# Newton's S as 32 moving columns, B's forms from PSUM, and k's DMA transpose ahead of C's transpose

## The chip, the cores and the metric

The kernel runs on one core of a Trainium2 chip. The metric is device time in microseconds (us); every time is the median of several executions, with the lowest and highest where they matter. A program on one core has one span per execution. The profile is of one execution, and the span of an execution is about 2 us shorter than its time (269.7 and 271.84 in the profiled one of the kernel before).

Short names: PE is the matmul engine (TensorE), PEld its weight loads, DVE is VectorE, ACT is ScalarE, POOL is GpSimd, SP issues DMA.

## The reference

Eight batches of eight heads, 576 tokens, head size 64. Attention in Nystrom form with 32 landmarks, then a gated feed-forward stage:

```python
q_lm = q.reshape(B, H, m, S // m, D).mean(axis=3)        # m = 32 landmarks
k_lm = k.reshape(B, H, m, S // m, D).mean(axis=3)
A, Bm, C = sm(q, k_lm), sm(q_lm, k_lm), sm(q_lm, k)      # sm: scaled softmax
Z = Bm.transpose(0, 1, 3, 2) / (norm1(Bm) * norm_inf(Bm) + 1e-06)
for _ in range(6):
    Z = 2 * Z - Z @ Bm @ Z                               # Newton
x = A @ Z @ C @ v                                        # then heads side by side: 4608 x 512
out = (1 / (1 + exp(-(x @ w_gate))) * (x @ w_val)) @ w_out   # d_ff = 1536
```

## The kernel before

Attention's work of batch b+1 is woven into the feed-forward matmuls of batch b (tiles gp, vp, then op). Who decides the weave matters for all that follows: while the program is built, a small model of the engines' times (class Model in the kernel) says when each piece's data will be there, and a loop puts the next piece on the PE when the model says that it is due. On the chip the order is fixed; if the model was wrong, PE stands at the matmul that it put too early.

```python
def start(self, engine, outs, ins):
    return max([self.free[engine]] + [self.landed.get(_handle(x), 0.0) for x in ins]
               + [self.waits.get(_handle(x), 0.0) for x in outs])
...
# in weave(): the first stream whose data the model has ready now; else the one that is ready first
now = model.free["pe"] + SLACK
...
SLACK, LAG, FILL = 0.02, 20, 1.0
```

The model knows when an operand has landed, when its engine is free and when a bank's former user is done. It does not know that two engines may not use one PSUM bank at once.

In a late batch (2 to 7) B's softmax ran from exponentials in SBUF (E), was transposed on VectorE, and spread into block-diagonal form (bd, bdT), four heads of 32 in 128 columns:

```python
E = sb.tile([128, 2, m], FP32, name=f"E_{b}", tag="E")
act.activation(out=E, in_=bs, func=AF.Exp, scale=scale2)
... # rs = row sums of E, rr = 1 / rs
act.mul(out=Bc[:, g, :], in_=E[:, g, :], mul=rr[:, g:g + 1])
dve.transpose(out=Bt, in_=Bc)
... # spread(dst, src): dst[:, g] = blk * src[:, g], broadcast over the four heads
spread(bdT, Bt)
... # s0 = bdT' bdT per group g, 128 columns
spread(bd, Bc)
```

Newton moves the square S (128 columns, three quarters of them zeros) and y (64) together through PE, and one VectorE operation makes the next pair:

```python
for it in range(ITERS):
    lo = 0 if it < ITERS - 1 else 128
    yield need(sy, banks=1)
    pn = bank([128, 2, 128 + D - lo], FP32, f"pn_{b}_{it}")
    for g in range(2):
        mm(out=pn[:, g, :], lhsT=sy[:, g, 0:128], rhs=sy[:, g, lo:128 + D], ...)
    dve.scalar_tensor_tensor(out=nsy, in0=sy, scalar=2.0, in1=pn, op0=ALU.mult, op1=ALU.subtract)
```

From batch 3 on k and q are transposed by DMA, and so is C (tile ct, from cl). Before, k's transpose of the next batch was issued after C's transpose of this one.

The softmax here doesn't subtract the row's maximum and nothing guards it: scores larger than these inputs give would overflow.

## Time and profile before

| | before |
|---|---|
| time | 271.59 us, median of 3 (271.58 to 271.88) |
| span in the profile | 269.7 us |
| granted TensorE clock | 0.998 |
| PE, DVE, ACT busy | 96%, 72%, 59% |

The busy shares and the chain that ended last are shown in the prediction. In the chain the first column is the start in us and the second the length; in the groups the two numbers after the bar are busy us in all and mean ns of one, and the last is the idle time of that engine just before them.

### The profile page before, as it was taken

How to read it: one execution, taken by the hardware profiler on the slowest of the kernel's cores; microseconds unless marked ns; L12 is line 12 of the kernel's file. 1: busy time of each engine (PE TensorE's matmuls, PEld its weight loads, DVE VectorE, ACT ScalarE, POOL GpSimd, SP SyncE). 2: the span in 40 equal slices, each digit the busy share in tenths (PEclk: the TensorE clock that was granted, in tenths of full speed). 3: DMA queues.
4: the chain of work that ended last, by engine and by line, in shares of the span. 5: the costliest groups of instructions: out<-in, count | busy, mean ns of one | idle time of the engine just before them, and what ended most of it. 6: DMA issues, size and time to landing. Idle time of an engine off the chain costs nothing.

```text
span 269.7 us, 8019 instructions
## 1 busy us (share of the span) xinstructions
PE 260.1 (96%) x3089; PEld 167.0 (62%) x3123; DVE 193.3 (72%) x551; ACT 159.4 (59%) x413; POOL 96.2 (36%) x107
## 2 busy tenths in 40 slices
PE   8999999999999999999999999999999999999994
PEld 5877777757664666556646665556636664665443
DVE  4566888976899788948986778848968786963111
ACT  3663876866647754876477655875368643964001
POOL 8523231960874039511953078212922000000000
PEclk9999999999999999999999999999999999999999
DMA  6999999999795998889794989589530413101433
GB/s 94 193 206 205 205 206 206 205 203 172 141 194 115 204 170 121 181 135 199 141 221 72 182 157 203 129 139 199 124 90 12 97 41 80 41 0 41 117 103 92
DMA packets 62645, 38.00 MB, mean 141 GB/s; under 512 B 33552, under 2 KB 58128, under 8 KB 62608
## 3 DMA queue, kind: packets, MB, share of 16 engines
q0 software_dynamic: 23600, 18.88, 47.0%
q1 hardware_dynamic: 38896, 18.52, 31.4%
q8 instruction: 24, 0.39, 0.6%
q14 instruction: 13, 0.11, 0.1%
q10 hardware_dynamic: 112, 0.10, 0.1%
HBM read 37.75 MB, written 9.44 MB: 175 GB/s over the span
## 4 chain that ended last, share of the span: by engine, by line
PE 93%; ACT 2%; issue 2%; POOL 1%; DVE 0%; POOLq 0%; ACTq 0%
PE op L247 34%; PE gp L247 18%; PE vp L247 18%; PE idle_ps L247 3%; PE pn L247 2%; PE cv L247 2%; PE rb L247 2%; PE sc L247 1%; PE sa L247 1%; PE tp_q L252 1%; PE up_1g L247 1%; PE up_0g L247 1%; PE up_2g L247 1%; PE tp_k L252 1%; PE up_1v L247 1%
## 5 line engine op out<-in xcount | busy, mean ns | idle before, releaser
L247 PE MATMUL op<-wo_sb,ht 128*128 128x512 bf16 (+1 forms) x410 | 109.4, 373 | 2.1 <-issue 1.1
L153 ACT ACTIVATE th<-gp 128x288 bf16<-128x288 f32 x192 | 76.7, 415 | 48.4 <-PE gp L247 36.7
L153 DVE SCALAR_TENSOR_TENSOR ht<-th,vp 128x288 bf16<-128x288 bf16 x192 | 82.0, 448 | 21.9 <-ACT th L153 17.2
L247 PE MATMUL gp<-an,U 128*128 128x288 bf16 x384 | 78.5, 286 | 0.3
L247 PE MATMUL vp<-an,V 128*128 128x288 bf16 x384 | 78.4, 286 | 0.0
L247 PEld LDWEIGHTS <-ht 128*128 128x128 bf16 x444 | 39.9, 98 | 26.7 <-issue 5.8
L247 PEld LDWEIGHTS <-U 128*128 128x128 bf16 x384 | 35.9, 98 | 27.3 <-issue 2.5
L247 PEld LDWEIGHTS <-V 128*128 128x128 bf16 x384 | 37.5, 98 | 9.7 <-issue 0.2
L153 ACT ACTIVATE ob<-op 128x512 f32<-128x512 f32 (+1 forms) x31 | 18.2, 587 | 29.6 <-PE op L247 24.2
L153 DVE SCALAR_TENSOR_TENSOR sy<-sy,pn 128x384 bf16<-128x384 bf16 x35 | 19.2, 548 | 2.3 <-PE pn L247 1.9
L153 DVE TENSOR_SCALAR ob<-op 128x512 f32<-128x512 f32 (+2 forms) x7 | 4.2, 596 | 17.3 <-PE op L247 17.3
L247 PE MATMUL idle_ps<-idle_w 128*128 128x256 bf16 x86 | 14.8, 308 | 1.2 <-DVE idle_w L297 1.2
L247 PE MATMUL pn<-sy 128*128 128x192 bf16 (+1 forms) x84 | 13.1, 237 | 0.4 <-ACT kT L153 0.3
L153 DVE TENSOR_TENSOR an<-aexp,rb 128x384 bf16<-128x384 bf16 (+1 forms) x32 | 12.4, 446 | 0.3 <-PE rb L247 0.3
L247 PEld LDWEIGHTS <-sy 128*128 128x128 bf16 x88 | 8.1, 97 | 6.2 <-DVE sy L153 2.8
L153 ACT ACTIVATE aexp<-sa 128x288 bf16<-128x288 f32 x32 | 10.7, 418 | 1.5 <-PE sa L247 1.1
L247 PEld LDWEIGHTS <-idle_w 128*128 128x128 bf16 x86 | 8.5, 109 | 3.3 <-DVE idle_w L297 1.2
L247 PEld LDWEIGHTS <-WT 64*32 64x32 bf16 x384 | 3.8, 89 | 9.1 <-issue 6.6
L270 POOL DMA_DIRECT2D kn<-in_k_dram x9 | 7.0, 779 | 4.6 <-DMA wg_sb<-in_moe_w_gate_dram 2.1
L153 DVE CAST U<-up_0g 128x512 bf16<-128x512 f32 x8 | 5.5, 690 | 4.1 <-PE up_0g L247 4.1
L270 POOL DMA_DIRECT2D vn<-in_v_dram x8 | 6.3, 789 | 5.3 <-PE gp L247 4.5
L270 POOL DMA_DIRECT2D qn<-in_q_dram x9 | 6.8, 753 | 4.0 <-PE sm L247 2.2
(201 smaller groups left out, 349.7 us busy)
## 6 DMA issues: line engine op xcount, KB each, us to landing
vn<-in_v_dram POOLq DMA_DIRECT2D x8, 576.0 KB, 9.4
kn<-in_k_dram POOLq DMA_DIRECT2D x7, 576.0 KB, 8.1
qn<-in_q_dram POOLq DMA_DIRECT2D x7, 576.0 KB, 10.6
out_dram<-ob SPq DMA_DIRECT2D x53, 64.0 KB, 3.0
out_dram<-ob SPq DMA_DIRECT2D x17, 192.0 KB, 2.3
out_dram<-ob SPq DMA_DIRECT2D x18, 128.0 KB, 2.4
wg_sb<-in_moe_w_gate_dram POOLq DMA_DIRECT2D x3, 512.0 KB, 19.7
wv_sb<-in_moe_w_val_dram POOLq DMA_DIRECT2D x3, 512.0 KB, 21.0
```

What stands on the lines that cost most here:

```text
L153: f(**kw)
L247: nc.tensor.matmul(**kw)
L252: nc.tensor.transpose(**kw)
L270: nc.gpsimd.dma_start(out=t[:, hs], in_=src[b, hs].rearrange("h (p c) d -> p h (c d)", p=P6))
```

## The change

Three parts, all in the late batches (the third from batch 4 on). (1) Newton: only the 32 nonzero columns of S move, so a pair of pn matmuls has 96 columns each in place of 192; the price is that S must be spread again on VectorE after each step (sd), from a copy in PSUM (new). (2) B's forms: the exponentials stay in the PSUM tile bs, bd is made straight from them, and a matmul with a matrix of ones (four) replaces VectorE's transpose. (3) Queues: k's transpose by DMA and its sums on GpSimd come ahead of C's transpose of the batch before, and the loads move with them. A small piece more is in the edit: from batch 1 on the column maxima (cc) lie in the PSUM bank of n1. Every experiment that starts from the change keeps this piece and the constant four, so neither was tried alone.

```diff
+    COMPACT = 2
+    four = consts.tile([128, m], BF16, name="four")
...
-        for what in ("k", "q") if b >= TURN else ():
+        for what in ("k", "q") if TURN <= b <= SWAP else ():
+            yield from turned_by_dma(what)
         for what in ("k", "q"):
+            if b > SWAP:
+                if what == "q":
+                    yield made(turned_c, b - 1)
+                yield from turned_by_dma(what)
...
-        E = sb.tile([128, 2, m], FP32, name=f"E_{b}", tag="E")
+        late = b >= LATE
+        E = bs if late else sb.tile([128, 2, m], FP32, name=f"E_{b}", tag="E")
...
+        if late:
+            for g in range(2):
+                dve.scalar_tensor_tensor(
+                    out=bd[:, g], in0=E[:, g, None, :].to_broadcast([128, NP, m]),
+                    scalar=rr[:, g:g + 1], in1=blk, op0=ALU.mult, op1=ALU.mult)
+            yield need(bd, banks=1)
+            Bt = bank([128, 2, m], FP32, f"Bp_{b}")
+            for g in range(2):
+                mm(out=Bt[:, g], lhsT=bd[:, g], rhs=four, start=(g == 0), stop=(g == 1))
+        if b >= COMPACT:
+            Bs = sb.tile([128, 2, m], BF16, name=f"Bt_{b}", tag="Bt")
+            act.copy(out=Bs, in_=Bt)
...
-                    mm(out=pn[:, g, :], lhsT=sy[:, g, 0:128], rhs=sy[:, g, lo:128 + D],
+                    mm(out=pn[:, g, :], lhsT=sd[:, g], rhs=sy[:, g, lo:w + D],
...
+                        dve.scalar_tensor_tensor(
+                            out=new, in0=sy[:, :, 0:m], scalar=2.0, in1=pn[:, :, 0:m],
+                            op0=ALU.mult, op1=ALU.subtract)
...
+                        dve.tensor_mul(
+                            out=sd, in0=blk[:, None].to_broadcast([128, 2, NP, m]),
+                            in1=new[:, :, None, :].to_broadcast([128, 2, NP, m]))
...
-            if b > TURN:
+            if TURN < b <= SWAP:
                 yield made(turned_c, b - 1)
```

More of the change, by code (lines that the diff above doesn't have):

```diff
@@ L350 @@
     model.free["dve"], model.free["act"] = 5.4, 6.6
+    four = consts.tile([128, m], BF16, name="four")
+    nc.vector.tensor_reduce(
+        out=four, in_=ident.rearrange("p (i l) -> p l i", i=NP), axis=AX.X, op=ALU.max)
     front_of, sums_of, lm_of, value_of, mid_of, norm_of, an_of, uv_of, step_at = ({} for _ in range(9))
-    square_of, turned_c, q_of = {}, {}, {}
+    square_of, turned_c, q_of, sd_of = {}, {}, {}, {}
     def copy(out, in_):
@@ L410, in front, with turned_by_dma @@
         ends = {}
-        for what in ("k", "q") if b >= TURN else ():
+        def turned_by_dma(what):
             yield made(nat, (what, b))
@@ L419, in front @@
                 t, t.rearrange("p h (c x) -> p (h c) x", c=3), n, n.rearrange("p h d -> p (h d)"))
+        for what in ("k", "q") if TURN <= b <= SWAP else ():
+            yield from turned_by_dma(what)
         for what in ("k", "q"):
+            if b > SWAP:
+                if what == "q":
+                    yield made(turned_c, b - 1)
+                yield from turned_by_dma(what)
+                if what == "q" and b < B - 1:
+                    load(b + 1, "k")
             if b >= TURN:
@@ L454, in front @@
             pool.tensor_add(out=s2, in0=s1, in1=t[:, :, 2 * P6:3 * P6])
-            if b >= SWAP and what == "k" and b < B - 1:
+            if b == SWAP and what == "k":
                 load(b + 1, "k")
+                load(b + 1, "q")
+            elif b > SWAP and what == "q" and b < B - 1:
                 load(b + 1, "q")
@@ L610, in mid @@
                 act.mul(out=Bc[:, g, :], in_=E[:, g, :], mul=rr[:, g:g + 1])
-        Bt = sb.tile([128, 2, m], BF16, name=f"Bt_{b}", tag="Bt")
-        dve.transpose(out=Bt.rearrange("p g l -> p (g l)"), in_=Bc.rearrange("p g l -> p (g l)"))
         bdT = sb.tile([128, 2, NP, m], BF16, name=f"bdT_{b}", tag="bdT")
         bd = sb.tile([128, 2, NP, m], BF16, name=f"bd_{b}", tag="bd", bufs=3)
+        if late:
[7 more added lines that the diff above has]
+                mm(out=Bt[:, g], lhsT=bd[:, g], rhs=four, start=(g == 0), stop=(g == 1))
+        else:
+            Bt = sb.tile([128, 2, m], BF16, name=f"Bt_{b}", tag="Bt")
+            dve.transpose(out=Bt.rearrange("p g l -> p (g l)"), in_=Bc.rearrange("p g l -> p (g l)"))
+        if b >= COMPACT:
+            Bs = sb.tile([128, 2, m], BF16, name=f"Bt_{b}", tag="Bt")
+            act.copy(out=Bs, in_=Bt)
         def spread(dst, src):
+            if late:
+                return dve.tensor_mul(
+                    out=dst, in0=blk[:, None].to_broadcast([128, 2, NP, m]),
+                    in1=src[:, :, None, :].to_broadcast([128, 2, NP, m]))
             for g in range(2):
@@ L627, in mid @@
         yield need(model.landed[Bc.name] + (0.25 if b else 0.0), banks=1)
-        n1 = bank([128, 2, m], FP32, f"n1_{b}")
+        n1_cc = bank([128, 2 * m + 2], FP32, f"n1_{b}")
+        n1 = n1_cc[:, 0:2 * m].rearrange("p (g l) -> p g l", g=2)
         mm(out=n1, lhsT=blk, rhs=Bc, start=True, stop=(b > 0))
@@ L631, in mid @@
             mm(out=n1, lhsT=eps, rhs=idle_w[:, 0:2 * m], start=False, stop=True)
-        ce = sb.tile([128, 2], FP32, name=f"cc_{b}", tag="cc")
+        ce = n1_cc[:, 2 * m:] if b > 0 else sb.tile([128, 2], FP32, name=f"cc_{b}", tag="cc")
         dve.tensor_reduce(out=ce, in_=n1, axis=AX.X, op=ALU.max)
@@ L638, in mid @@
         dve.reciprocal(out=rc, in_=ce)
-        apart = 2 if b == 0 else 1
+        apart, w = 2 if b == 0 else 1, m if b >= COMPACT else 128
         yield need(bdT, banks=apart)
-        s0 = [bank([128, 2 // apart, 128], FP32, f"s0_{b}{x}") for x in range(apart)]
+        s0 = [bank([128, 2 // apart, w], FP32, f"s0_{b}{x}") for x in range(apart)]
         s0 = [s0[g % apart][:, g // apart] for g in range(2)]
         for g in range(2):
-            mm(out=s0[g], lhsT=bdT[:, g], rhs=bdT[:, g], start=(g == 0 or b == 0), stop=(g == 1 or b == 0))
-        sy = sb.tile([128, 2, 128 + D], BF16, name=f"sy_{b}_0", tag="sy0", bufs=2)
+            mm(out=s0[g], lhsT=bdT[:, g], rhs=Bs[:, g] if b >= COMPACT else bdT[:, g],
+               start=(g == 0 or b == 0), stop=(g == 1 or b == 0))
+        sy = sb.tile([128, 2, w + D], BF16, name=f"sy_{b}_0", tag="sy0", bufs=2)
         if b == 0:
             model.by_part.add(sy.name)
-        s_at = [each(b, g).mul(sy[:, g, 0:128], s0[g], rc[:, g:g + 1]) for g in range(2)]
+        s_at = [each(b, g).mul(sy[:, g, 0:w], s0[g], rc[:, g:g + 1]) for g in range(2)]
         if b == 0:
             square_of[b] = [(sy, s_at)]
-        spread(bd, Bc)
+        elif b >= COMPACT:
+            sd_of[b] = sb.tile([128, 2, NP, m], BF16, name=f"sd_{b}_0", tag="sd", bufs=2)
+            for g in range(2):
+                dve.scalar_tensor_tensor(
+                    out=sd_of[b][:, g], in0=s0[g][:, None, :].to_broadcast([128, NP, m]),
+                    scalar=rc[:, g:g + 1], in1=blk, op0=ALU.mult, op1=ALU.mult)
+        if not late:
+            spread(bd, Bc)
         aexp = sb.tile([128, 2, S], BF16, name=f"aexp_{b}", tag="aexp", bufs=2)
@@ L667, in scale_y @@
                 dve.tensor_mul(out=ysc, in0=rcs, in1=rc)
-                y_at = [each(b, g).mul(sy[:, g, 128:128 + D], cv[g], ysc[:, g:g + 1])
+                y_at = [each(b, g).mul(sy[:, g, w:w + D], cv[g], ysc[:, g:g + 1])
                         for g in range(2)]
@@ L671, in scale_y @@
                 y_at = [dve.tensor_scalar(
-                    out=sy[:, g, 128:128 + D], in0=cv[g], scalar1=rcs[:, g:g + 1],
+                    out=sy[:, g, w:w + D], in0=cv[g], scalar1=rcs[:, g:g + 1],
                     scalar2=rc[:, g:g + 1], op0=ALU.mult, op1=ALU.mult) for g in range(2)]
@@ L802, in newton @@
             sy, bd, _ = mid_of[b]
+            compact = b >= COMPACT
+            w = m if compact else 128
+            sd = sd_of.pop(b) if compact else sy[:, :, 0:128]
             y6 = sb.tile([128, 2, 2, D], BF16, name=f"y6_{b}", tag="y6")
             for it in range(ITERS):
-                lo = 0 if it < ITERS - 1 else 128
-                yield need(sy, banks=1)
-                pn = bank([128, 2, 128 + D - lo], FP32, f"pn_{b}_{it}")
+                last = it == ITERS - 1
+                lo = w if last else 0
+                yield need(sy, *((sd,) if compact else ()), banks=1)
+                p = bank([128, 2 * (w + D - lo) + 2 * m * (compact and not last)], FP32, f"pn_{b}_{it}")
+                pn = p[:, 0:2 * (w + D - lo)].rearrange("p (g x) -> p g x", g=2)
                 for g in range(2):
-                    mm(out=pn[:, g, :], lhsT=sy[:, g, 0:128], rhs=sy[:, g, lo:128 + D],
+                    mm(out=pn[:, g, :], lhsT=sd[:, g], rhs=sy[:, g, lo:w + D],
                        start=(g == 0), stop=(g == 1))
-                if lo == 0:
-                    nsy = sb.tile([128, 2, 128 + D], BF16, name=f"sy_{b}_{it + 1}", tag="sy", bufs=3)
+                if not last:
+                    if compact:
+                        new = p[:, 2 * (w + D):].rearrange("p (g x) -> p g x", g=2)
+                        dve.scalar_tensor_tensor(
+                            out=new, in0=sy[:, :, 0:m], scalar=2.0, in1=pn[:, :, 0:m],
+                            op0=ALU.mult, op1=ALU.subtract)
+                    nsy = sb.tile([128, 2, w + D], BF16, name=f"sy_{b}_{it + 1}", tag="sy", bufs=3)
                     dve.scalar_tensor_tensor(
                         out=nsy, in0=sy, scalar=2.0, in1=pn, op0=ALU.mult, op1=ALU.subtract)
+                    if compact:
+                        sd = sb.tile([128, 2, NP, m], BF16, name=f"sd_{b}_{it + 1}", tag="sd", bufs=2)
+                        dve.tensor_mul(
+                            out=sd, in0=blk[:, None].to_broadcast([128, 2, NP, m]),
+                            in1=new[:, :, None, :].to_broadcast([128, 2, NP, m]))
+                    else:
+                        sd = nsy[:, :, 0:128]
                     sy = nsy
@@ L820, in newton @@
                             out=y6[:, g],
-                            in0=sy[:, g, None, 128:128 + D].to_broadcast([128, 2, D]), scalar=2.0,
+                            in0=sy[:, g, None, w:w + D].to_broadcast([128, 2, D]), scalar=2.0,
                             in1=pn[:, g, None, :].to_broadcast([128, 2, D]),
```

## The prediction

> **What bounds the kernel now.** I read the page first, for the busy shares and the chain that ended last; then the sums by 10 us windows; then the chain piece by piece in one steady stretch; then TensorE's and VectorE's groups kept apart by shape; last the list of waits.
>
> ```profile
> span 269.7 us, 8019 instructions
> PE 260.1 (96%) x3089; PEld 167.0 (62%) x3123; DVE 193.3 (72%) x551; ACT 159.4 (59%) x413; POOL 96.2 (36%) x107
> PE 93%; ACT 2%; issue 2%; POOL 1%; DVE 0%; POOLq 0%; ACTq 0%
> ```
>
> The reader sees a TensorE kernel: PE is busy 96% and carries 93% of the chain. The other 7% lies nearly all before 50 us, where the first batch is being loaded and warming matmuls (idle_ps, 86 of them) fill the gaps. After that PE has no holes, as the chain shows around the sixth of eight batches:
>
> ```profile
> 131.07 0.43 PE op L247 x2
> 131.51 0.19 PE pn L247 x2
> 133.60 0.17 PE pn L247 x2
> 134.69 0.06 PE pn L247 x2
> 135.66 0.11 PE wtp L247 x2
> 136.70 0.34 PE up_0g L247 x8
> 137.04 0.22 PE up_0v L247 x8
> 138.78 0.97 PE op L247 x4
> 140.90 0.43 PE op L247 x2
> ```
>
> (These are picked lines of one stretch.) A pair of 512-column matmuls takes 0.43 us, a pair of 192 columns 0.17, of 128 columns 0.11, of 64 columns 0.06: PE runs at its streaming rate, about 0.42 ns a column, and the price of a matmul is its moving columns. The one other cost is a change between whole-array matmuls and those in 32-column tiles: the first group of eight after a change takes 0.34 us where the next takes 0.22, and four op take 0.97 after a change back where two pairs need 0.86. So each edge costs 0.11 to 0.12 us.
>
> Does PE wait for anybody in the loop that the change rewrites (Newton, tiles pn and sy)?
>
> ```profile
> PEld L247 <- DVE sy L153: 3.1, 12, 0.4
> DVE sy L153 <- PE pn L247: 1.9, 6, 0.7
> L247 PE MATMUL pn<-sy 128*128 128x192 bf16 x70 | 11.5, 246 | 0.4 <-ACT kT L153 0.3
> ```
>
> The weight loads wait 3.1 us in all, but the matmuls behind them see 0.4 us of idle: other work of the feed-forward stage lies between two Newton steps and hides the VectorE round trip. VectorE's groups that I use for sizes:
>
> ```profile
> L153 DVE SCALAR_TENSOR_TENSOR sy<-sy,pn 128x384 bf16<-128x384 bf16 x35 | 19.2, 548 | 2.3 <-PE pn L247 1.9
> L153 DVE TENSOR_TENSOR an<-aexp,rb 128x192 bf16<-128x192 bf16 x16 | 5.5, 346 | 0.0
> L153 DVE SCALAR_TENSOR_TENSOR y<-sy,pn 128x128 bf16<-128x128 bf16 x14 | 3.4, 283 | 0.9 <-PE pn L247 0.7
> L153 DVE STREAM_TRANSPOSE Bt<-Bc 128x64 bf16<-128x64 bf16 x8 | 2.0, 246 | 4.4 <-ACT Bc L153 4.3
> L153 DVE TENSOR_SCALAR sy<-s,rc 128x128 bf16<-128x128 f32 x15 | 4.6, 345 | 0.6
> ```
>
> **What the Trainium skill says.** "VectorE: DVE Perf Modes", section "Why PSUM operands drop a tier": a PSUM operand in fp32 leaves a two-tensor operation at one element a cycle. The trace agrees: 384, 192 and 128 elements in 548, 346 and 283 ns are close to 148 ns plus n/0.96. So I take 215 ns for 64 elements and 415 for 256. "TensorE: Matmul & The Clock Gate", section "Back-to-back issue gap", puts a floor of about 60 cycles (25 ns) under a matmul of up to 64 columns; the trace agrees (the 96 x 32 sums lm_0k and the 64-column pn both follow each other by about 28 ns), so a matmul of 32 columns is no cheaper than one of 64. "TensorEngine Tiling (Array Packing)", section "Key Properties", says that a change of tiling mode drains TensorE; the trace shows it as the 0.11 us edge above.
>
> **The change part by part.** On the PE, in columns.
> Newton: six batches (2 to 7) times five steps times two matmuls go from 192 to 96 columns. A pair cost 0.17 us and should cost 0.085: 30 pairs times 0.085 = 2.5 us saved. The sixth step stays at 64 columns.
> The starting square s0: six pairs of 128 columns (0.11) become pairs of 32 at the floor (0.06): 0.3 saved.
> B's transpose: six pairs with the new matrix of ones ("four"), 32 columns, at the floor: 6 x 0.06 = 0.35 added.
> Edges: I counted them in the order of the built programs, taking whole array, 64-row tiles and 96-row tiles as three modes: 94 before, 103 after (in the late batches C's scores now come with B's ahead of the up-projection, and the A scores and C's value product are no longer neighbours). 9 x 0.11 = 1.0 us added.
> Warming matmuls stay 86, and the order of batches 0 and 1 stays; the one extra reduction in the setup (about 0.25 us of VectorE) lies beside ScalarE's 1.16 us copy of sel, which the chain runs through. I count nothing for it.
> Sum on the path: -2.5 - 0.3 + 0.35 + 1.0 = -1.45 us.
>
> On VectorE, which is beside the path. A Newton step was one operation of 384 elements (548 ns, the next starting some 0.47 us after it). It becomes three: 64 elements into PSUM (215), which the next must wait for, then 192 (348) and 256 (415); with the overlap of the last two that is 0.85 us. 0.38 more, times 30 = 11.4 us. For B and s0 per batch: the transpose goes (-0.25), the two spreads become one of the same size, bd's two become slower ones from PSUM with a scalar (+0.2), s0's two get shorter (-0.2) and two new ones of 128 elements appear (+0.6): about 0.4, times 6 = 2.3. VectorE goes from 193 to about 207 us, 77% of the span. ScalarE takes six small copies, 1.4 us in all. None of this is on the path as long as PE has other work between two Newton steps.
>
> The moves on the queues (k's transpose and its GpSimd sums ahead of C's transpose, k's load behind q's transpose) make landmarks ready earlier. PE waits for none of that now, so the move by itself earns nothing; it lets the order put a batch's attention work every 26 us of PE work, where it was 29.5.
>
> **Rivals.**
> VectorE becomes the bound. For: per batch it had about 22 us of work in 29.5, and gets about 24 in 26, and during Newton it is nearly full already. Against: counted in the built order for batch 4, PE has 9.8 us of work between its first and last Newton pair (6.3 before), and VectorE about 10.2 (7.0 before): the ratio is better than before, where PE hardly waited. If it fails, each of six batches could stall PE by 0.5 to 1 us: 273 to 276.
> A transfer becomes the bound. For: the tighter period gives loads, transposes and the two half-swaps less time, and PE's order is fixed. Against: in batches 4 to 7 the queries' landmarks were ready about 2 us before the B scores that use them, and DMA is idle in much of the last third. One stall of 1 us in each late batch would give 273 or so.
> The round trip hides nothing and the PE saving is lost to the edges and small waits: 271 to 271.6, the same as before.
> A larger gain than the columns (below 268) would need waits that I cannot find after 50 us, or a shorter start; the start is not touched.
>
> **Range and chances.** 271.6 - 1.45 = 270.1; I add 0.3 for small waits at the longer Newton round trip: 270.4. The best case is about 269 (no edges felt, columns fully earned), a bad one 272.5, with one rival partly true. 8 in 10: 269.0 to 272.2. Faster by over 2% means below 266.2, which the columns cannot pay: 2%. Slower by over 2% means above 277, six stalls of a microsecond: 4%. The rest, 94%, is within 2%.
>
> **What would show it.** The pn pairs of late batches take 0.08 to 0.09 us in the chain, in place of 0.17; the busy time of pn falls by some 2 us or more; VectorE's busy time is near 207; the edges cost 0.11 each; the share of PE in the chain stays at 93%. I am wrong if PE shows idle before pn, bs or up in the late batches (VectorE or a transfer took over), if the new VectorE operation into PSUM takes much more than 0.22 us, or if the stretch before 50 us changes its length.

## The result, and the profile after

The changed kernel took 273.13 us (median of 4, 272.95 to 273.56), and the kernel before took 271.63 us (median of 4, 271.58 to 271.88) beside it. The ratio is 1.0056, with a 95% interval of 1.0038 to 1.0073: slower by half a per cent, within 2%, and above the predicted range. A ratio here is the mean time of one kernel's fast runs over that of the other's of the same rounds, so it is not quite the ratio of the medians.

First the head of the page of the changed kernel (span, busy time of the engines, shares of the chain by engine):

```profile
span 270.8 us, 8170 instructions
...
PE 263.0 (97%) x3135; PEld 164.3 (61%) x3135; DVE 201.4 (74%) x612; ACT 160.9 (59%) x419; POOL 96.2 (36%) x107
...
PE 89%; ACT 4%; DMA 3%; DVE 2%; issue 1%; POOL 1%; ACTq 0%; POOLq 0%
```

Two lines disagree at first sight: PE is busier, 97% against 96%, yet its share in the chain fell from 93% to 89%. The chain points the right way: between 50 us and the last gp it holds 11.3 us of ScalarE and VectorE, and none before. It is no measure of the loss, for PE worked through most of these 11.3 us; and its 3% of DMA is the first load of q, which took the place of other pieces before 10 us. The busy share misleads. A matmul's record lasts longer than its turn (rtp below has a record of 246 ns, and a matmul of its 128 columns follows the one before by 55 ns), so a wait of 0.2 us disappears under the tail of the matmul before it; besides, 34 of the 444 op matmuls had no record in the profile before and all have one here. The Trainium skill, "Perfetto Trace Analysis", section "Identifying the Most-Contended Engine", says that matmul busy share is no good measure of how close a kernel is to its limit; this pair of profiles agrees, since the share rises by a point while the kernel gets slower. So I compared the starts of the matmuls instead.

The groups of the changed kernel, kept apart by shape, show what the new pieces cost:

```profile
L153 DVE TENSOR_TENSOR sd<-blk,pn 128x256 bf16<-128x256 bf16 x30 | 12.4, 415 | 0.0
L153 DVE SCALAR_TENSOR_TENSOR sy<-sy,pn 128x192 bf16<-128x192 bf16 x30 | 10.6, 354 | 1.0
L153 DVE SCALAR_TENSOR_TENSOR pn<-sy,pn 128x64 f32<-128x64 bf16 x30 | 6.6, 222 | 0.1
L153 DVE SCALAR_TENSOR_TENSOR bd<-bs,rr,blk 128x128 bf16<-128x128 f32 x12 | 3.7, 346 | 3.6 <-ACT Bc L153 3.6
L249 PE MATMUL pn<-sy,sd 128*128 128x96 bf16 x60 | 7.5, 207 | 0.1
L254 PE MATMUL rtp<-ident,rhl 128*80 128x128 bf16 x8 | 2.0, 246 | 0.2
```

The first three rows are the new Newton step on VectorE, with close to the durations predicted (415, 348, 215 ns). The pn row has 7.5 us of busy time for 60 matmuls, where the wide one had 11.5 for 70 (ten of them, batch 1's, stay wide and take 1.7). The bd row is the surprise: VectorE stood 3.6 us in front of twelve operations, released by ScalarE's Bc, from which bd takes no data.

**Where the time went.** I took the start of every matmul from the two traces and put them against the order of the built program. Each matmul was given its columns at the streaming rate (2.38 columns a ns, at least 27 ns) and each change of tile mode 0.1 us; call the sum the work. What a stretch takes beyond its work is called lost. This is an estimate from the trace's own rates, the same for both kernels.

| us | before | after |
|---|---|---|
| PE work of the whole program | 251.4 | 249.9 |
| lost up to the end of batch 0's gp and vp | 10.05 | 10.06 |
| lost from there to the last gp of batch 7 | 4.10 | 6.79 |
| start of the last pair of gp | 245.31 | 246.50 |

The work fell by 1.5 us, as predicted. The loss in the start did not change. But 2.7 us more are lost in the steady part, and 2.7 - 1.5 = 1.2 is what the profiled run lost (1.19 at the last pair of gp, 1.1 in the span).

The largest single piece is at 65.9 us, in batch 2. The chain of the changed kernel there (start, length, what):

```profile
65.15 0.86 ACT cexp L153 x2
66.02 0.36 ACT Bc L153 x2
66.37 0.02 issue
66.40 0.04 DVE bd L153
66.43 0.23 issue
66.67 0.35 DVE bd L153
67.02 0.05 issue
67.07 0.19 PE Bp L249
```

and three lines of its timeline (what stands in brackets is the idle time of the engine before the line, and who ended it):

```profile
65.91 0.46 ACT L153 ACTIVATE Bc<-bs,rr 128x32 bf16<-128x32 f32 x2
...
66.40 0.61 DVE L153 SCALAR_TENSOR_TENSOR bd<-bs,rr,blk 128x128 bf16<-128x128 f32 x2 [0.88 <-ACT Bc L153]
...
66.81 0.45 PE L249 MATMUL Bp<-four,bd 128*128 128x32 bf16 x2 [0.50 <-DVE bd L153]
```

ScalarE has C's exponentials (cexp) to do first; its Bc comes after them. VectorE's bd reads the same PSUM tile bs, so the built program lets it wait for Bc, and PE's Bp waits for bd: 0.66 us at the first Bp by the starts and 0.23 at the second. The Trainium skill, "PSUM — Partial Sum Buffer", section "PSUM bank collisions raise a hardware error", says that the hardware doesn't arbitrate between two engines on one bank, reads included, and that they must be ordered by semaphores. The trace agrees in so far as the built program orders them: bd is released by ACT Bc six times (3.6 us in all), with no data between them. What happens without that order, no run here shows. The kernel's model does not know this, so it put Bp too early.

The other waits are small: 0.21 us at each of four row-sum transposes (rtp of batches 3 to 6), 0.19 before pn in two batches, 0.15 after n1 in two, 0.1 each in three other places. All that I can name add to 3.0 us after. Before they add to between 0.5 and 1.4, as some of its gaps may be missing records. The rest of the 6.8 and the 4.1 is spread too thin to name.

The chain at an rtp shows what these are made of:

```profile
97.49 1.01 ACT aexp L153 x3
98.50 0.31 ACT th L153
98.81 0.02 issue
98.83 0.04 DVE ht L153
98.87 0.34 issue
99.20 0.42 DVE sm L153
99.62 0.02 issue
99.65 0.21 DVE rhl L153
...
100.14 0.25 PE rtp L254
```

ScalarE does A's exponentials (aexp), then th; VectorE's next operation in line is ht, which needs th, and the row sums' reciprocal (sm) and rhl stand behind it. VectorE was idle for 1.27 us ahead of that ht:

```profile
98.83 0.46 DVE L153 SCALAR_TENSOR_TENSOR ht<-th,vp 128x288 bf16<-128x288 bf16 x1 [1.27 <-ACT th L153]
```

So VectorE is not full there: it stands in line for ScalarE. That points to the order; experiments have to show it.

### The profile page after: what moved, and what is told of

Same layout as the page of the kernel before. It is cut to its first block, busy times and chain, and to the rows that moved or that the text cites. A ratio compares the mean times of both kernels' runs of the same rounds, so it can differ in the third digit from the quotient of the medians.

```text
span 270.8 us, 8170 instructions
## 1 busy us (share of the span) xinstructions
PE 263.0 (97%) x3135; PEld 164.3 (61%) x3135; DVE 201.4 (74%) x612; ACT 160.9 (59%) x419; POOL 96.2 (36%) x107
## 4 chain that ended last, share of the span: by engine, by line
PE 89%; ACT 4%; DMA 3%; DVE 2%; issue 1%; POOL 1%; ACTq 0%; POOLq 0%
PE op L249 35%; PE gp L249 16%; PE vp L249 16%; DMA qn<-in_q_dram 3%; PE idle_ps L249 2%; ACT aexp L153 2%; PE pn L249 2%; PE rb L249 2%; PE sc L249 1%; PE tp_q L254 1%; PE sa L249 1%; PE up_0g L249 1%; PE up_2g L249 1%; PE up_1g L249 1%; PE cv L249 1%
## 5 line engine op out<-in xcount | busy, mean ns | idle before, releaser
L249 PE MATMUL op<-wo_sb,ht 128*128 128x512 bf16 (+1 forms) x444 | 112.7, 374 | 0.0
L153 DVE SCALAR_TENSOR_TENSOR ht<-th,vp 128x288 bf16<-128x288 bf16 x192 | 79.8, 449 | 19.1 <-ACT th L153 18.3
L249 PEld LDWEIGHTS <-ht 128*128 128x128 bf16 x444 | 39.9, 98 | 32.4 <-issue 7.1
L249 PEld LDWEIGHTS <-U 128*128 128x128 bf16 x384 | 35.0, 98 | 20.0 <-issue 0.8
L153 ACT ACTIVATE ob<-op 128x512 f32<-128x512 f32 (+1 forms) x29 | 17.1, 589 | 28.6 <-PE op L249 25.2
L153 DVE TENSOR_SCALAR ob<-op 128x512 f32<-128x512 f32 (+2 forms) x9 | 5.5, 616 | 19.8 <-PE op L249 19.8
L153 DVE SCALAR_TENSOR_TENSOR sy<-sy,pn 128x192 bf16<-128x192 bf16 (+1 forms) x35 | 13.3, 381 | 1.7 <-PE pn L249 0.7
L153 DVE TENSOR_TENSOR sd<-blk,pn 128x256 bf16<-128x256 bf16 x30 | 12.4, 415 | 0.0
L249 PEld LDWEIGHTS <-sd 128*128 128x128 bf16 x72 | 6.3, 98 | 7.9 <-DVE sd L153 2.4
L249 PE MATMUL pn<-sy,sd 128*128 128x96 bf16 (+1 forms) x72 | 8.9, 205 | 0.1
L153 ACT ACTIVATE cl<-sl 128x288 bf16<-128x288 f32 x20 | 7.9, 414 | 1.3 <-PE sl L249 1.1
```

The lines of the kernel that those rows point to most:

```text
L153: f(**kw)
L249: nc.tensor.matmul(**kw)
```

## The experiments

Three theories. The *order theory*: PE's order is fixed at build by the kernel's own model, the order before happened to fit the chip, and any part that moves the order loses time in small waits, whatever the part itself costs. The *VectorE theory* (the first rival of the prediction): the longer Newton step on VectorE makes PE wait, so kernels with VectorE's old load do not lose. The *transfer theory*: the moved transposes and loads come late. Under the last two the loss belongs to one part and goes with it. The expectations number them: theory 1 is the wait of bd for Bc on the shared PSUM tile, which the model doesn't know, 2 the VectorE theory, 3 the transfer theory, 4 the order theory.

Each edit is told against the changed kernel, save two against the kernel before. "Lost" is as defined above, from the profiled run, in the steady part (before 4.1, after 6.8); "work" is PE's. All runs gave correct results.

**One part left out.** Five rounds in one call; before 271.69 (271.46 to 272.86, 11 runs).

```diff
# e1_forms_as_before: B's forms as before
-        late = b >= LATE
+        late = False
-            Bs = sb.tile([128, 2, m], BF16, name=f"Bt_{b}", tag="Bt")
-            act.copy(out=Bs, in_=Bt)
+            Bs = Bt
# e2_wide_newton: Newton as before
-    COMPACT = 2
+    COMPACT = 99
# e3_queues_as_before: transposes and loads as before
-        for what in ("k", "q") if TURN <= b <= SWAP else ():
+        for what in ("k", "q") if TURN <= b else ():
-            if b > SWAP:
+            if False:
-            if TURN < b <= SWAP:
+            if TURN < b:
... # and both loads after k's sums
```

> B's forms as in the kernel before (exponentials in SBUF, VectorE's block transpose), narrow Newton and the new queue order kept. In the built order PE has 248.6 us of work by my count (249.9 in the change, 251.4 before) and 93 edges (103 in the change). Theory 1, VectorE's new block-diagonal B waits for ScalarE on a shared PSUM tile and PE's order does not know: the 0.9 us stall of batch 2 goes, with 1.3 us of work: about 270.9 us. Theory 2, VectorE is too full in the Newton stretch: only 0.4 us per batch leaves VectorE, the other stalls (about 1.9 us) stay, about 271.8 us.

> Newton's S with 128 columns and one VectorE operation a step as before; B's forms from PSUM and the new queue order kept. PE work by count 252.1 us (2.1 more than the change). Theory 1: batch 2's stall at B's transpose stays; about 275 us. Theory 2, VectorE too full: stalls of 2.3 us vanish with the 2 us per batch that leave VectorE: about 272.9 us, no slower than the change.

> Loads, transposes and their order as before; narrow Newton and B's forms from PSUM kept. PE work by count 249.0 us, 94 edges. Theory 1: batch 2's stall stays (its order is not touched by the queues), the small later ones too: 0.9 us less work, about 272.2 us. Theory 3, the tighter period that the queue order brings makes the later stalls: these (about 1.4 us) vanish too, about 270.8 us.

Measured: without the forms 272.05 us, ratio to before 1.0015 (0.9982 to 1.0048), lost 7.7; with wide Newton 276.34, ratio 1.0168 (1.0150 to 1.0187), lost 8.1; with the old queues 274.26, ratio 1.0096 (1.0073 to 1.0120), lost 9.4. Leaving out a part never brings the loss back to 4.1, and leaving out the narrow Newton or the queues makes the kernel slower than the whole change. The medians lie 0.25, 1.3 and 2.1 us above the highest time that any theory had expected for the three. Where the waits lie changes from kernel to kernel: without the forms 0.5 and 0.7 us stand ahead of B's and C's scores of batch 5 (bs and sl, behind a GpSimd operation, bq); with wide Newton 0.4 to 0.9 us stand at Bp in five batches (2 and 4 to 7) and 0.9 ahead of cv of batch 3. One wait does go with its part: the 0.9 us at Bp of batch 2 stand in the traces of all kernels with that batch's bd read from PSUM and the model not told (the change, e2, e3, e5), and in none of the others.

**The model told more.** In the same call, one kernel whose model is told of the shared tile and of a scalar column's cost. The instructions are the change's.

```diff
# e7_told
-            columns = sum(k in aps for k in ("scalar1", "scalar2", "mul"))
+            columns = sum(k in aps for k in ("scalar", "scalar1", "scalar2", "mul"))
+            model.waits[bd.name] = model.landed[Bc.name]
+                model.waits[bdT.name] = model.landed[Bs.name]
```

> The change with only its order of emission told the truth: the scheduler's model learns that VectorE's block-diagonal B starts after ScalarE's normalised B, that its spread starts after ScalarE's copy of the transpose, and that a scalar column costs 60 ns in the three-operand form. The instructions are the same, their order is not. PE work by count 248.9 us, 93 edges. Theory 1: the stalls at B's transpose vanish and about 1 us of work with them: about 271.0 us or a little less. Theory 2: VectorE's load is the same, stalls of about 2 us stay somewhere: 272.1 us or more.

Measured: 272.76 us, ratio 1.0044 (1.0015 to 1.0073), work 248.9, lost 8.6. Work fell by 1.0 because the new order has 93 mode changes in place of 103, but more is lost. The wait at Bp of batch 2 is gone, but others came (0.5 and 0.7 us between C's scores, for example). The model told three things does not give an order that fits better on the whole; telling it one of them is tried below.

**One part alone.** Four rounds; before 271.70 (271.28 to 275.87, 9 runs). The edits are pairs of those above: Newton alone is e1 and e3 together, the forms alone e2 and e3, the queues alone e1 and e2.

> Only the narrow Newton of the change; B's forms and the queues as before. PE work by count 249.1 us (2.3 less than before), VectorE 12 us more. Theory 2 (VectorE's load makes PE wait): about 2 us or more of waits, 271.3 us or more. Theory 4 (the order of before is finely fitted to the chip, and any change of the order brings waits of 2 to 5 us, whatever VectorE's load): the same here, 271.5 to 274; it is told apart by the next two, which have VectorE's load of before.

> Only B's forms from PSUM; Newton and queues as before. PE work by count 251.9 us (0.4 more), VectorE about 1 us more. Theory 1: the 0.9 us stall of batch 2 and smaller ones in later batches at B's transpose: about 273.2 us. Theory 2: no waits elsewhere. Theory 4: waits of 2 us or more, also at places without B's forms.

> Only the new order of loads and transposes; Newton and B's forms as before. PE work by count 251.2 us (0.2 less), VectorE's load as before. Theory 2: no new waits, 271.4 us. Theory 3 (the tighter period) and theory 4 (any new order): waits of 1 to 4 us, 272.5 us or more.

Measured: Newton alone 272.98 us, ratio 1.0042 (1.0021 to 1.0064), lost 7.6; the forms alone 275.30, ratio 1.0148 (1.0114 to 1.0181), lost 7.1; the queues alone 275.03, ratio 1.0127 (1.0092 to 1.0162), lost 8.5. Alone, the three cost 0.4, 1.5 and 1.3%, which is 3.2% in sum; together they cost 0.6%. They do not add, so most of the loss is not a fixed property of a part.

The queues alone lose time without VectorE's new work. The head of its page:

```profile
PE 263.3 (96%) x3123; PEld 168.5 (62%) x3123; DVE 193.1 (70%) x551; ACT 159.0 (58%) x414; POOL 96.0 (35%) x107
```

VectorE has exactly its old work (193 us, 551 instructions), and PE loses 4.4 us more than before. What it waits for most is a transfer. The view of the tile ct (C's transpose), first its own row, then what PE waited for ahead of cv, which reads it (us, times):

```profile
L389 SPq DMA_TRANSPOSE ct<-cl x5: 1428/1576/2242, 90.2 to 201.6; - x5
...
  DMA ct<-cl: 7.2, 4
```

and the same view of the changed kernel:

```profile
L389 SPq DMA_TRANSPOSE ct<-cl x5: 1466/1820/3136, 88.9 to 197.6; - x5
its engine sat idle before it (us, times) until:
  issue: 0.2, 1
```

(The 7.2 us are over weight loads and matmuls, so most of it is counted twice; by the starts, cv of batches 4 and 5 waits 1.45 and 2.18 us.) These two waits are 3.6 of the 4.4 us. From its issue to its landing the slowest ct takes 8.7 us here, 7.2 in the change and 5.1 before. That the moved queue is the reason is not shown: p1 below has the old queue, and a ct of 8.6 us. In the whole change PE does not wait at cv. So a late transfer is the loss of this kernel, and not that of the change.

**The wait of batch 2 taken away, same order.** If the shared PSUM tile makes bd wait, exponentials in SBUF free it. The order of instructions on all five engines is that of the change, so only the wait differs. One kernel does it in all late batches (in the call of "one part alone"), one in batch 2 only.

```diff
# e8_e_in_sbuf
-        E = bs if late else sb.tile([128, 2, m], FP32, name=f"E_{b}", tag="E")
+        E = sb.tile([128, 2, m], FP32, name=f"E_{b}", tag="E")
# g2_e_in_sbuf_batch_2
+        E = bs if late and b > 2 else sb.tile([128, 2, m], FP32, name=f"E_{b}", tag="E")
```

> The whole change, but with the exponentials of B in SBUF in place of PSUM, so that VectorE and ScalarE need not take turns on one PSUM tile. The order of the instructions stays the same on every engine, nothing else changes. Theory 1: VectorE no longer waits for ScalarE there and the 0.9 us at B's transpose in batch 2 shrinks to 0.3 or less: 0.6 to 0.9 us faster than the change, about 272.4 us. If the stall comes of ScalarE or VectorE being late anyway, no difference.

Measured: 274.07 us (273.07 to 276.51), ratio 1.0100 (1.0049 to 1.0151), lost 7.0. In batch 2 the wait is gone (lost from bs to the first pn 0.8 us in place of 1.5), but in batch 6 the same stretch loses 2.0 us in place of 0.7; a new wait of about 1 us stands at Bp there, which comes behind bd and a copy that stands in line after it. The timeline of this kernel shows why (VectorE and GpSimd):

```profile
169.87 1.64 POOL L153 TENSOR_TENSOR s_7k<-kT 128x768 f32<-128x768 bf16 x1 [2.65 <-DMA kT<-kn]
...
170.94 2.44 DVE L153 SCALAR_TENSOR_TENSOR bd<-E,rr,blk 128x128 bf16<-128x128 f32 x2
...
171.59 1.64 POOL L153 TENSOR_TENSOR s_7k<-s_7k,kT 128x768 f32<-128x768 f32 x1
```

and the second bd alone:

```profile
171.58 1.80 DVE L153 SCALAR_TENSOR_TENSOR bd<-E,rr,blk 128x128 bf16<-128x128 f32 x1
```

Two bd operations take 2.44 us where they take 0.61 elsewhere. The first lasts until just after GpSimd's first addition (it ends at 171.66, the addition at 171.51); the second lasts 1.80 us, until just after GpSimd's second addition, which ends at 173.23. Both of bd's tensors now lie in SBUF. The Trainium skill, "SBUF — State Buffer", section "SBUF: two separate sides", says that VectorE with two SBUF inputs and a GpSimd operation that reads SBUF share one pair of ports, and that whoever starts first holds it for the whole instruction. The trace agrees: 1799 ns against 344 (which of the two started first it can't tell, the records are 7 ns apart). With bs in PSUM, as the change has it, bd escapes this, though it meets such additions too:

```profile
172.31 1.64 POOL L153 TENSOR_TENSOR s_7k<-kT 128x768 f32<-128x768 bf16 x1 [3.78 <-DMA kT<-kn]
172.56 0.61 DVE L153 SCALAR_TENSOR_TENSOR bd<-bs,rr,blk 128x128 bf16<-128x128 f32 x2 [0.54 <-ACT Bc L153]
```

> The change with B's exponentials in SBUF in batch 2 alone; the order on all engines as in the change. Theory 1: VectorE's block-diagonal B no longer waits for ScalarE there, PE's wait of 0.9 us at B's transpose of batch 2 shrinks to 0.1 or nothing, and everything behind it comes 0.8 us earlier: 0.8 us under the change. If another wait takes it up later: no difference at the end.

Measured, five rounds, before 271.57: 272.95 us, ratio 1.0048 (1.0019 to 1.0077), beside the change itself (label c1_after) at 273.15, ratio 1.0057 (1.0031 to 1.0083). In the trace the wait is gone: bd starts at 65.69 and no wait is marked at Bp.

```profile
65.69 0.61 DVE L153 SCALAR_TENSOR_TENSOR bd<-E,rr,blk 128x128 bf16<-128x128 f32 x2
...
66.33 0.22 PE L249 MATMUL Bp<-four,bd 128*128 128x32 bf16 x2
```

Lost is 6.2 in place of 6.7 in the change of the same call. So the wait is shown to come of the shared tile: in the stretch from bs to the first pn it cost 0.7 us. Its price in the time of the whole kernel is not shown: 0.2 us between the medians is less than the intervals resolve.

> The change once more, unaltered, as the control beside the kernel above: 273.1 to 274.6 us, as in its two earlier runs.

Measured: as told, 273.15 us. The change repeats.

**The kernel before with another order.** Nothing but one constant of the weave is changed in the kernel before; all instructions stay. If the order alone can cost microseconds, this shows it. Four rounds; before 271.72 (271.38 to 275.20, 9 runs).

```diff
# p1_before_lag, against the kernel before
-    SLACK, LAG, FILL = 0.02, 20, 1.0
+    SLACK, LAG, FILL = 0.02, 22, 1.0
# p3_before_slack, against the kernel before
-    SLACK, LAG, FILL = 0.02, 20, 1.0
+    SLACK, LAG, FILL = 0.03, 20, 1.0
```

> No part of the change: the kernel before with one constant of its scheduler moved (the lag of the second feed-forward stage, 20 to 22). The instructions are the same and as many (251.4 us of PE work by count, 94 edges), the loads of all engines too; about half of PE's order shifts a little. Theory 2 (VectorE's load) and theory 3 (the queues): no change, 271.7 us. Theory 4 (the order of before is fitted to the chip, and any other order brings waits): 273 us or more.

> A second one of the same kind: the kernel before with the scheduler's slack at 0.03 us in place of 0.02. Same instructions but for one warming matmul, order shifted from early on. Theory 4: 272.5 us or more. Otherwise 271.7 us.

Measured: LAG 22 gives 278.35 us (275.51 to 280.58, one of the five slow, that is over 1.5% above the fastest), ratio 1.0191 (1.0119 to 1.0262, so slower, but unclear whether by 2%), work 251.4 as before, lost 8.1. SLACK 0.03 gives 271.83, ratio 0.9985 (0.9936 to 1.0033), lost 4.3; the order theory had expected 272.5 or more, so this one missed. The two are not equally large moves: compared line by line with the order before, 3104 of 3122 matmuls keep their sequence with SLACK 0.03, and 2770 of 3123 with LAG 22 (in the change it is 2271 of 3135). The chain of the first shows the largest of its waits, again C's transpose:

```profile
149.95 8.55 DMA ct<-cl
158.50 0.04 issue
158.55 0.56 PE cv L247 x48
```

The same instructions in another order lose 4.0 us more, with VectorE's and ScalarE's old work. That is more than the change lost. But it is not the same kind of loss: by the starts, about 2.4 us of it stand ahead of cv (1.94 in batch 5) and 1.5 at A's scores (sa) of batch 2, behind VectorE, while the change has many small waits. So the kernel before sits at a good point among these three settings, and an order can cost microseconds by itself; that the change's small waits come of its order is made likely by this, not shown.

**The model told one thing.** If the order is at fault, an order made with the missing fact should be better.

```diff
# f1_forms_from_3: batch 2 keeps the old forms of B
-        late = b >= LATE
+        late = b > LATE
... # Bs = Bt in batch 2, copied from PSUM after it
# f4_told_bd, and again as f4_again: bd comes after Bc
+            model.waits[bd.name] = model.landed[Bc.name]
# f5_told_bd_rtp: f4, and rtp asked for later
-        yield need(rhl, banks=1)
+        yield need(model.landed[rhl.name] + 0.3, banks=1)
# f9_told_bd_slack: f4, and more slack
-    SLACK, LAG, FILL = 0.02, 20, 1.0
+    SLACK, LAG, FILL = 0.03, 20, 1.0
```

> The change, but with B's forms from PSUM from batch 3 on in place of 2: batch 2, whose C scores fill ScalarE just then, has B's forms as before. PE work by count 249.8 us, 102 edges. Theory 1: batch 2's 0.9 us stall goes; about 272.2 us. If new waits come of the shifted order (theory 4), 272.5 to 274 us.

> The change, its scheduler told one thing alone: VectorE's block-diagonal B starts after ScalarE's normalised B. Same instructions; PE work by count 249.0 us, 94 edges. Theory 1: 0.9 us of stall and 0.9 us of edges less than the change, about 271.3 us. Theory 4: the stall of batch 2 goes, others come; 272 us or more.

Measured in the call of the two kernels above: f1 273.71 us (271.10 to 275.09), ratio 1.0018 (0.9952 to 1.0084), lost 8.0; f4 271.96 (271.39 to 273.51), ratio 0.9996 (0.9945 to 1.0047), lost 6.5. In f1 the wait at Bp is gone, but 0.9 and 0.7 us stand at bs and sl of batch 6. (The clock of its profiled run was 0.991, but low only before 12 us, ahead of the part in which loss is counted.) In f4 bd still waits for Bc as long as in the change, but PE asks for Bp later and does not wait (timeline of f4):

```profile
65.61 0.46 ACT L153 ACTIVATE Bc<-bs,rr 128x32 bf16<-128x32 f32 x2
...
66.09 0.61 DVE L153 SCALAR_TENSOR_TENSOR bd<-bs,rr,blk 128x128 bf16<-128x128 f32 x2 [0.88 <-ACT Bc L153]
...
66.76 0.20 PE L249 MATMUL Bp<-four,bd 128*128 128x32 bf16 x2
```

A last call put it beside the change, with two variations: five rounds, before 271.90 (271.09 to 272.55, 11 runs).

> The change itself again, on the chip of the next three. 273.1 us, 1.0055 of before.

> The change told that VectorE's block-diagonal B starts after ScalarE's normalised B, again, beside the change. Theory 1 and the edges: 1.0 to 1.5 us faster than the change, 271.8 us; if the first run was luck, 273.

> The same, and the transpose of the row sums asked for 0.3 us later, so that PE meets it after VectorE has finished. PE work by count 248.6 us, 90 edges. If the small waits at the row sums are worth their 0.8 us: about 271 us. If they only move elsewhere: 271.5 to 273 us.

> The kernel of f4_again with the scheduler's slack at 0.03 in place of 0.02: one warming matmul less, the same other instructions in another order. Theory 4: differs from f4_again by 0.5 us or more in either direction; otherwise the same, 271.8 us.

Measured:

| | median us | ratio to before (95%) | work | lost |
|---|---|---|---|---|
| c0_after (the change) | 274.59 | 1.0101 (1.0071 to 1.0131) | 249.9 | 7.2 |
| f4_again | 271.81 | 0.9989 (0.9966 to 1.0012) | 249.0 | 6.6 |
| f5_told_bd_rtp | 272.88 | 1.0025 (0.9994 to 1.0056) | 248.6 | 6.8 |
| f9_told_bd_slack | 272.86 | 1.0036 (1.0013 to 1.0059) | 248.9 | 7.1 |

(One run each of f4_again, f5 and f9 was slow; it counts in the median and not in the ratio.)

One line in the model, with the instructions of the change, makes the kernel 1.1% faster than the change in this call (1.0101 / 0.9989) and equal to the kernel before. In its two other calls the change had 1.0056 and 1.0057, which would make it 0.6 to 0.7%. By the traces 0.9 us of it is work: the new order has 94 mode changes, not 103. Only 0.3 to 0.6 us of it is less waiting; the wait at Bp went, others (0.45 us between gp and vp, 0.55 at an op) came. Asking for rtp later (f5) removes the waits at rtp, but Newton's pn waits in their place, and nothing is gained. SLACK 0.03, which cost the kernel before nothing, takes f9's ratio 0.5% above f4's, as the order theory had expected. No kernel of this study clearly beats the kernel before.

**What stays open.** The runs of the change and its variants scatter more than those of the kernel before (the change: 272.95 to 273.56 in one call, 272.98 to 276.20 in another), with granted clocks from 0.993 to 1.0 and no rule that I found; the profiled runs of the change lie at the low end, so the extra microseconds of the others have no trace. A part of the scatter can be seen in two other traces: in e5 (0.994) and f1 (0.991) the clock was 0.50 for 3.4 us near 10 us, and the first gp started at 32.6 and 32.4 us, where it started between 30.6 and 31.2 in the three traces of the change. But runs at 1.0 are scattered too (272.98 to 275.06 in c0_after). Of the 2.7 us, one part (the shared tile in batch 2, 0.7 us by two traces with the same order, 0.9 by the starts) has a shown cause. The rest is many waits of 0.1 to 0.2 us. That another order can cost as much is shown by p1, whose waits are others; that these small ones come with the order, and what the model has wrong at each of them, was not shown.

## Why the prediction was wrong

The prediction was 270.4 us with a range of 269.0 to 272.2; the result is 273.13.

- *The columns on PE (-2.5, -0.3, +0.35): right.* A pn pair takes 0.09 us in the chain (at 129.15 and 131.18 us of the changed kernel, for example), against 0.17 before and 0.085 predicted.

```profile
129.15 0.09 PE pn L249 x2
...
131.18 0.10 PE pn L249 x2
```

- *The edges (+1.0): right.* 103 in the built order. The sum of the work, -1.45 predicted, is -1.5 by the starts; f4, which has nine fewer and is faster, is in step with it.
- *VectorE's operations: right.* 222, 354 and 415 ns against 215, 348 and 415. Its busy total is 201.4, not 207. The rows themselves came: the three of Newton sum to 29.6 us where thirty wide steps had 16.5 (19.2 less the 2.7 of batch 1's five). All records of VectorE together last 16.0 us longer, but they overlap, and the total, which counts an overlap once, rose by 8.1.
- *"PE waits for none of that now, so the move by itself earns nothing": half right.* It earns nothing, but by itself it costs 1.3% (e6): PE then waits 3.6 us at cv for two late transposes. What makes them late stays open.
- *"I add 0.3 for small waits at the longer Newton round trip": this is the step that failed.* The term measured 2.7 us, and for the most part not at Newton: pn's waits are about 0.5 of it. The prediction had its waits at Newton alone, and carried over from the kernel before that PE hardly waits elsewhere, as if that belonged to its load. What the runs showed in its place: bd waits on ScalarE for a PSUM tile that the two share, unknown to the model (0.9 us at Bp of batch 2), and four waits of 0.21 us at rtp and some smaller ones, whose cause stays open. p1 shows that PE's few waits need not outlive a change of order alone. The order is recomputed at build, and the profile before can't say how well a new one will fit. Of its own signs of being wrong, PE idle before pn showed faintly (two waits of 0.19 us), the largest wait stood at Bp, which it hadn't named, and PE's share in the chain fell to 89% where it was to stay at 93%.
- *The rival "VectorE becomes the bound" would have named a size close to the result (273 to 276), but for a reason that the runs do not bear out:* with wide Newton (e2) the loss stays at 8.1, and VectorE stands idle ahead of the late bd and rhl. The waits at pn, about 0.5 us, may still be its share.
- *The rival "a transfer becomes the bound"* is not what happened in the change; in e6 and p1 a late transfer is the largest loss.
- *The start was not touched:* right, 10.05 and 10.06 us lost up to the same point.

A better prediction would have been 271.6 - 1.45 plus an allowance for a new order. By these runs of this one kernel that allowance lies between 2 and 5 us: lost rises from 4.1 to between 6.5 and 9.4 in all the kernels with a new order, but for p3 (4.3), which hardly moves it.

## What to carry to other kernels

In a kernel whose order is fixed at build by a model of the chip, the kernel before is one tuned point; a change that saves work also draws a new order, and its waits are a cost of their own; in p1 they came to 4 us with no instruction changed. So before judging such a change, tell the model what is new in it (here: two engines on one PSUM bank take turns), compare it with a reordered kernel before as a control, and read the starts of the matmuls, as the busy share of PE hides waits of 0.2 us. Moving a tile to PSUM trades one neighbour for another: the wait for the other engine on the bank against the wait for GpSimd on SBUF's shared ports.

## What the Trainium skill lacked or had wrong

- "TensorE: Matmul & The Clock Gate", section "Back-to-back issue gap", gives some 131 ns a matmul of 512 columns and some 81 ns of 128 as sustained in a real kernel. Here a pair of 512 columns takes 0.43 us (215 ns each) and a pair of 128 takes 0.11 us (55 ns each), which is its figure for an isolated matmul.
- "TensorEngine Tiling (Array Packing)", section "Key Properties", says that a mode change drains TensorE and gives no amount: 0.11 to 0.12 us at each end here.
- "PSUM — Partial Sum Buffer" says that two engines must be ordered on a bank, not what it costs: VectorE idle 0.88 us in batch 2 and 3.6 us over six batches.
- "SBUF — State Buffer" describes VectorE and GpSimd blocking each other and gives a ratio that was measured, but no times for a small operation: 1799 ns in place of 344 when a GpSimd addition of 1.64 us ran.
- "Perfetto Trace Analysis" offers, beside the useful share of peak (MFU), the weight loads' busy share instead of the matmuls'. That share did not show the loss either (62% before, 61% after, with PE's work 1.5 us smaller); the starts of the matmuls did.
